# A recurrent attention block with a gated MLP behind it: the first batch's written order, its TensorE filler, the load of its states and one load's place in a queue

## Chip, cores and metric

The kernel runs on one core of a Trainium2 chip. The metric is the device time in microseconds (us) of one launch. The engines are TensorE (PE in the profile; PEld is its weight load), VectorE (DVE), ScalarE (ACT), GpSimd (POOL) and SyncE (SP), which here only issues DMAs.

## What is computed

```python
# x (8, 8, 512, 64), state (8, 8, 32, 64): batches, heads, tokens or states, width
scores  = scale * x @ state^T;  a  = softmax(scores,  -1);  xread = a @ state
scores2 = scale * state @ x^T;  a2 = softmax(scores2, -1);  sread = a2 @ x
y = concat([xread, sread], axis=2)     # 544 rows for each batch and head
y = y.transpose(0, 2, 1, 3).reshape(4352, 512)
h = y @ w_in                           # w_in (512, 2048)
sp = max(h, 0) + log1p(exp(-|h|))
out = (h * erf(sp)) @ w_out            # w_out (2048, 512)
```

x, state and out are float32. The weights come as 64-bit floats and are turned into float32 on the chip, by integer and float operations on the two words of each number.

## The kernel before

**Tiling.** All is done batch by batch, 512 tokens at a time. xread is never formed: the state of a batch is first multiplied by w_in (a "mixed" weight m, 32 states by 512 columns for each head), and the softmax weights aT then go against m. The 2048 hidden columns are cut into four groups of 512 (g or o in the code); each group's hidden values are made, go through softplus, erf and a product, and are projected by w_out into four PSUM accumulators of 128 tokens (o0 to o3). Batches 1 to 7 and the state rows use a seven-product scheme (hidden_wide L469, project_wide L610, hidden_states L527, project7 L587); the first batch does plain products.

**The first batch is a written list.** The string order0 (L1018 to L1039) holds step names; each name is a function in the dictionary do, made by step and copied (L742, L745), and running through the list emits the instructions. in_order (L81) then fixes this order on each of PE, DVE, ACT and SP, so on every engine a step can't pass the one named before it. A suffix _a puts a PSUM copy on ACT (L747), _v on DVE (L748). The names that matter:

- wN: N filler products of 128x128 (warm, L191 to L196) into a PSUM bank nobody reads.
- x0 to x3: transposes of two heads of x each (turn, L766, matmul at L770); x0_v, x1_a and so on copy them to xT. st: transposes of the first batch's states (turn_st, L775, L778), copied by st_v to st00.
- s0, s1: scores of four heads each (score, L781, matmul at L788); s00_a, s01_a, s10_a, s11_a copy them out of the two banks. tm0, tm1 turn them to tokens in rows (L795) into the two PSUM buffers named at.
- max, less, exp, sum, inv, norm with 0 or 1: softmax (L816 to L823). ta0, ta1 turn the weights (L801), ta0_a and ta1_a copy them to aT.
- i0 to i7 and o0 to o7: pieces of w_in and w_out (pieces, L731). Each has two ACT steps (a0 at L167, a1 at L169) and three DVE steps (v0 at L172, v1 at L173, v2 at L174); i0 is done in two halves, the second written i0+. get (L936) asks for the next piece from DRAM; a piece lands in one of three raw buffers, so piece n+3 can be asked for only when the v2 step of piece n is done.
- mGF: mixed weights of group G from column block F on (mixed_part, L868, matmul at L877), which takes two at buffers; mGFk_a or _v copies one half. hGI: hidden block I of group G (first, L881, matmul at L887; a third digit means one half of it). softGI, erfGI (erfGI+ for two blocks), mulGI: L917, L922, L924. pGRI: projection of block I into accumulator R (second, L890, matmul at L894). putR: copy (L900) and store of accumulator R.
- u0, u1: transposes of the other batches' states (L866). big, wt, wz, wn, tw, read: the second softmax and sread. q..., n..., cm..., ca..., lxq, lx, kept: work for batch 1, with its loads.

**Queues.** Nearly all DMAs are issued by SP, in program order. At the start these are x of batch 0 (L115, two of the four from ACT), the state of batch 0 twice (L120, once for each half of the columns, so that one transpose of 128 columns gives both halves of the partitions), three pieces of weights (L157), and the states of batches 1 to 7 (load_st, L123, L126). load_xq (L97, L102) loads the queries of a batch with 16 DMAs.

**After the first batch.** The loop over n (L1097) runs two steps for each batch 1 to 7. At n = 0 the accumulators 2 and 3 of batch 0 are still being stored: excursion(1, ..., 2, ...) does sread of batch 1, mixed weights, and attention(2), and attention(b) (L300) ends its scores with load_xq(b + 1), here load_xq(3), 16 DMAs. The two stores put2 and put3 follow (L1158, L1159). The output tile ot has three buffers, used in turn: put2, then o1, then o2 of project_wide share one ring, so that the tile o2 of n = 0 takes the buffer of put2 and o1 of n = 0 that of an earlier store. The next output additions are at L616, on DVE.

Of the kernel before, what the change touches and what calls it, by code (L numbers as in the profile page):

```python
# [9 lines left out]
F32 = mybir.dt.float32  # L10
# [7 lines left out]
def kernel(  # L18
# [17 lines left out]
    nc = tc.nc  # L36
# [70 lines left out]

    st = const.tile([P, B, P], F32, name="st")
    away0 = ring[:, 1, 0].rearrange("p k i t -> p (k i t)")
    st0 = away0[:, 512:768].rearrange("p (g k d) -> p g k d", g=2, k=2)  # L110
    x0 = xin.tile([P, NC, H, D], F32, name="x").rearrange("p c h d -> p (c h d)").rearrange(
        "p (h c d) -> p h c d", h=H, c=NC)
    x_t[0] = x0.rearrange("p h c d -> p c h d")
    for i in range(NI):
        (nc.scalar, nc.sync)[i % 2].dma_start(  # L115
            out=x0[:, 2 * i:2 * i + 2].rearrange("p h c d -> p h (c d)"),
            in_=x[0, 2 * i:2 * i + 2].rearrange("h (p c) d -> p h (c d)", c=NC))
        if i == 1:
            for k in range(2):
                nc.sync.dma_start(out=st0[:, :, k],  # L120
                                  in_=state[0].rearrange("(g h) n d -> (h n) g d", g=2))

    def load_st():  # L123
        for h in range(H):
# [63 lines left out]

    spare = ps_h.tile([P, S], F32, name="h")

    def warm(n):  # L191

        for _ in range(n):
            last = nc.tensor.matmul(out=spare[:, 0:P], lhsT=ident, rhs=ident, start=True,
                                    stop=True)
        return last  # L196

# [102 lines left out]
    def attention(b, xT, *pool, held=None):  # L300

        if held is None:
            held = {"sc": scores(b, xT, *pool)[0]}
            if b + 1 < B:
                load_xq(b + 1)
        sc = lambda e: held["sc"][:, e]
        tt = nc.vector.tensor_tensor
        turn, both = nc.vector.transpose, lambda: d["both"]
        d = {}
        a = lambda e: both()[:, e].rearrange("p (k n) -> p k n", n=Ns)  # L310

        def begin():
            d["both"] = att.tile([P, NI, S], F32, name="xT")
            d["m1"], d["z1"] = (small.tile([P, 2, NC * NI], F32, name=n) for n in ("m1", "z1"))
            d["m2"], d["z2"] = (small.tile([P, 2], F32, name=n) for n in ("m2", "z2"))
            aT[b] = keep.tile([P, 2, S], F32, name="aT")
    
        def most():
            for e in range(2):
                yield lambda e=e: (d or begin(),  # L320
                                   turn(out=both()[:, e], in_=sc(e)))
            for e in range(2):
                yield lambda e=e: nc.vector.reduce_max(out=d["m1"][:, e], in_=a(e), axis=AX.X)
            for e in range(2):
                yield lambda e=e: tt(a(e), a(e), over(d["m1"][:, e]), op=ALU.subtract)
            for e in range(2):
                yield lambda e=e: nc.vector.reduce_max(out=d["m2"][:, e:e + 1], in_=sc(e),
                                                       axis=AX.X)
            yield lambda: nc.vector.tensor_scalar(d["m2"], d["m2"], -scale, None, op0=ALU.mult)

        def exps():
            for e in range(2):
                yield lambda e=e: nc.scalar.activation(out=a(e), in_=a(e), func=ACTF.Exp,
                                                       scale=scale)
            for e in range(2):
                yield lambda e=e: nc.scalar.activation(
                    out=both()[:, 2 + e], in_=sc(e), func=ACTF.Exp, bias=d["m2"][:, e:e + 1],
                    scale=scale, accum_out=d["z2"][:, e:e + 1])

        def total():  # L340
            for e in range(2):
                yield lambda e=e: nc.vector.reduce_sum(out=d["z1"][:, e], in_=a(e), axis=AX.X)
            yield lambda: (inverse(d["z1"]), inverse(d["z2"]))

        def ready():
            for e in range(2):
                yield lambda e=e: tt(a(e), a(e), over(d["z1"][:, e]), op=ALU.mult)
            for e in range(2):
                yield lambda e=e: turn(out=aT[b][:, e], in_=both()[:, e])
            for e in range(2):  # L350
                yield lambda e=e: (turn(out=both()[:, e], in_=both()[:, 2 + e]),
                                   send() if e else None)

        def send():
            a2T = d["a2T"] = att.tile([P, 2, NC, P], F32, name="sc")
            blocks = both()[:, 0:2].rearrange("p e (c m n) -> p m (e c) n", m=NI, n=Ns)
            rows = a2T.rearrange("p e c (i n) -> p i (e c) n", n=Ns)
            for m in range(NI):
# [391 lines left out]
    def start0():  # L750
# [24 lines left out]
        def turn_st():  # L775
            held["st"] = ps_h.tile([P, 2 * P], F32, name="h")
            for g in range(2):
                nc.tensor.transpose(out=held["st"][:, P * g:P * g + P],  # L778
                                    in_=st0[:, g].rearrange("p k d -> p (k d)"), identity=ident)

        def score(g):  # L781
            if not nat:
# [73 lines left out]
    def groups0():  # L856
# [8 lines left out]
            for n, b in enumerate(bs):  # L865
                nc.tensor.transpose(out=ps_s[k][:, n], in_=st[:, b, :], identity=ident)  # L866

        def mixed_part(g, first, n):  # L868
            if (0, g) not in m_t:
                m_t[0, g] = mix.tile([P, 2, gw], F32, name="m")  # L870
            ps = ps_m[g, first] = [ps_at.tile([P, gw], F32, name="at")[:, 0:n * P]
                                   for _ in range(2)]
            for h in range(H):
                i, e = h // 2, h % 2
                r = slice(D * e, D * e + D)
                k, p = where[h]
# [29 lines left out]
        for g in range(NG):  # L906
            for first_, n in ((0, 1), (1, 1), (2, 2)) if g == 0 else ((0, 2), (2, 2)):
                step("m%d%d" % (g, first_), mixed_part, g, first_, n)
                for k in range(2):
                    copied("m%d%d%d_" % (g, first_, k),  # L910
                           lambda g=g, f=first_, n=n, k=k: m_t[0, g][:, k, P * f:P * (f + n)],
# [96 lines left out]
    for _ in range(3):  # L1008
        fetch()
    load_st()  # L1010
    for n in 8, 12:
        step("w%d" % n, warm, n)
    start0()
    groups0()
# [1 line left out]
    ready = next0()  # L1016

    order0 = """  # L1018
        w8 x1 x1_v i0a0 i0a1 x0 x0_v i0v0 i0+a1 i0+a0 st st_v i0v1 x2 x2_v x3 x3_a s0 s00_a i0+v0
        i0v2 s1 i0+v1 i0+v2 s01_a s10_a tm0 max0 less0 s11_a tm1 exp0 w12 max1 less1 sum0 i1a0  # L1020
        inv0 norm0 exp1 o0a0 m01 sum1 m011_a u0 m010_a i1a1 ta0 ta0_a inv1 norm1 m00 ta1 big1
        i1v0 m000_a get i1v1 i1v2 m001_a h000 ta1_a h01 u0_v o0v0 m02 m020_v h001 u1 m021_v h03
        h02 o1a1 o0a1 soft01 o0v1 o0v2 u1_v lxq1 soft00 erf00+ mul00 mul01 p030 get o1a0 p020
        o1v0 o1v1 o1v2 soft03 get p000 soft02 erf02+ mul02 i2a0 mul03 p001 i2a1 p010 i2v0 p031
        i2v1 i2v2 p021 i3a0 i3a1 i3v0 p002 p011 get p003 o2a1 big0 big p032 o2a0 wt0 m10 m100_v
        p012 wt1 p013 m101_v h11 soft11 h10 soft10 i3v1 i3v2 m12 m121_a xq1v wz p033 p022 wn0
        p023 o2v0 m120_v h13 o2v1 o2v2 h12 erf10+ mul10 get o3a1 wn1 get mul11 o3a0 o3v0 o3v1
        p110 soft13 soft12 o3v2 p111 erf12+ mul12 i4a0 i4a1 get get i5a0 p100 p101 p130 p131 p132
        mul13 tw0 tw0_a i4v0 i5a1 i4v1 i4v2 p102 p112 m20 m201_a m200_a p120 i5v0 i5v1 p121 p122
        h20 i5v2 o4a0 o4v0 get m22 m221_v m220_v get h21 o4a1 o4v1 o4v2 tw1 tw1_v h22 soft20 o5a0  # L1030
        o5v0 h23 p133 p123 o5a1 soft21 erf20 mul20 erf21 soft23 soft22 o5v1 mul21 p103 erf22 p200
        o5v2 p201 p220 get erf23 mul22 mul23 i6a0 i6v0 i6a1 i6v1 read read_v p113 i7a0 i7v0 i6v2
        p210 get get q q1_v p221 p230 qm1 o6a0 q0_a qm0 m30 o6v0 p222 o6a1 m301_v i7a1 p211
        m300_a o6v1 o6v2 n1 n10_a n11_v qm7 cm0 h30 n0 n01_a i7v1 qm6 h31 lx1 soft31 soft30 p202
        p203 i7v2 qm8 erf30 n00_v kept cm2 cm1 cm3 m32 m320_a p223 p231 p232 mul30 qm2 erf31 p233
        p330 m321_a qe3 h33 qm3 mul31 lxq2 o7a0 qm4 o7v0 get get p331 h32 qe2 qm5 p300 p301 qe1
        qs1 qe0 qs0 p320 p321 qs2 qr0 qr2 soft33 erf33 p212 qr1 p213 p310 p311 o7a1 ca0 qr3
        soft32 erf32 ca2 mul33 ca1 ca3 o7v1 o7v2 get mul32
    """  # L1039
    steps0 = order0.split()  # L1040
    for n, name in enumerate(steps0):
# [55 lines left out]
    for n, (b, u) in enumerate((b, u) for b in range(1, B) for u in range(2)):  # L1097
# [57 lines left out]
        if n == 0:  # L1155
            done(steps)
            excursion(1, (1, sets(1 - begins(1))), 2, lambda: erf_part(inner, inside))
            for r in 2, 3:  # L1158
                do["put%d" % r]()  # L1159
        if n == 0:  # L1160
            times_part(inner, slice(0, 1))
            times_part(inner, slice(3, 4))
# [122 lines left out]
```

## Time and profile before

| | |
|---|---|
| runs, device us | 722.75, 724.76, 1508.96 (median 724.76) |
| profiled execution: device us, span us | 722.23, 720.4 |
| granted TensorE clock, mean | 0.995 |
| all 896 + 672 matmuls of L631 | 203.0 + 161.4 us busy, 379 and 381 ns each |
| DMA | 74.70 MB, mean 104 GB/s; HBM read 49.87 MB, written 20.45 MB |

The profiled execution has its own time, 722.23 us, of which the span from its first to its last instruction is 720.4 us; 1.8 us lie outside it. A float32 product shows as two MATMUL records and a transpose as one. Matmuls overlap in the record, so sums of their durations exceed the time they take: a 128x512 record starts 0.43 us after the one before it, a 128x256 record 0.216 us, a 128x128 record 0.11 us at full clock and 0.213 us at half clock. DVE and ACT rows are start, busy time, and the wait ahead of them in brackets.

### The profile page before, as it was taken

To read this page: it belongs to the slowest core of one execution; us is meant where nothing else is said; L and a number is where in the kernel's file an instruction comes from. 1 tells how busy PE (TensorE), PEld (TensorE's weight loads), DVE (VectorE), ACT (ScalarE), POOL (GpSimd) and SP (SyncE) were. 2 spreads that over 40 slices of the span, in tenths; PEclk is the share of its full clock that TensorE was granted. 3 is DMA by queue.
4 is the path that set the end of the run, shared out by engine and by line. 5 is a ranking of instruction groups with operands and counts; after the bars stand their busy time and mean duration, and the time that the engine had idled before them with its cause. 6 is when DMAs were issued, how large, how long until landed. Compare 5 with 4: busy or idle time off the path is not lost.

```text
span 720.4 us, 10904 instructions
## 1 busy us (share of the span) xinstructions
PE 708.6 (98%) x4257; PEld 561.2 (78%) x4257; DVE 542.0 (75%) x877; ACT 374.8 (52%) x535; POOL 25.2 (3%) x34
## 2 busy tenths in 40 slices
PE   6999999999999999999999999999999999999997
PEld 6444347678878878887888878887888888889996
DVE  5897888879868988788776967697877757665533
ACT  4999695636464625545346436462464535342340
POOL 0000000000100000000000000000000000000000
PEclk8999999999999999999999999999999999999999
DMA  8956795650249163513723280615242321102101
GB/s 270 237 200 207 217 297 163 131 184 30 43 88 222 24 133 49 142 50 79 112 29 146 60 146 2 176 30 148 29 104 83 89 49 25 34 30 30 23 9 29
DMA packets 144339, 74.70 MB, mean 104 GB/s; under 512 B 123424, under 2 KB 132896, under 8 KB 142752
## 3 DMA queue, kind: packets, MB, share of 16 engines
q1 hardware_dynamic: 139520, 65.95, 33.1%
q0 software_dynamic: 4032, 7.34, 7.6%
q10 hardware_dynamic: 736, 0.72, 0.3%
q8 instruction: 33, 0.54, 0.3%
q14 instruction: 18, 0.15, 0.1%
HBM read 49.87 MB, written 20.45 MB: 98 GB/s over the span
## 4 chain that ended last, share of the span: by engine, by line
PE 89%; ACT 4%; DMA 2%; SPq 2%; DVE 2%; issue 1%; DVEq 0%; ACTq 0%
PE o L631 46%; PE h L489 13%; PE at L489 10%; PE o L894 5%; PE h L534 3%; PE o L606 3%; PE h L383 2%; PE at L383 1%; PE at L275 1%; SPq L102 1%; PE h L887 1%; ACT raw L169 1%; PE at L887 1%; DMA raw<-in_moe_w_in_dram 1%; DMA raw<-in_moe_w_out_dram 1%; SPq L75 1%
## 5 line engine op out<-in xcount | busy, mean ns | idle before, releaser
L631 PE MATMUL o<-w_out,ring 128*128 128x256 f32 x896 | 203.0, 379 | 0.0
L631 PEld LDWEIGHTS o<-w_out,ring 128*128 128x128 f32 x896 | 169.9, 190 | 24.8 <-DVE ring L1089 0.8
L631 PE MATMUL o<-raw,ring 128*128 128x256 f32 x672 | 161.4, 381 | 0.0
L631 PEld LDWEIGHTS o<-raw,ring 128*128 128x128 f32 x672 | 126.6, 190 | 25.8 <-ACT m L385 9.2
L482 ACT ACTIVATE ring<-ring 128x512 f32<-128x512 f32 x112 | 70.6, 631 | 60.5 <-DVE ring L472 59.9
L489 PE MATMUL h<-aT,m 128*128 128x256 f32 x336 | 82.2, 380 | 1.7 <-DVE ring L472 1.7
L1089 DVE TENSOR_TENSOR ring<-ring 128x1024 f32<-128x1024 f32 (+1 forms) x61 | 70.6, 1200 | 4.5 <-ACT ring L546 4.5
L489 PEld LDWEIGHTS h<-aT,m 128*128 128x128 f32 x336 | 63.7, 190 | 12.1 <-DVE ring L472 2.1
L472 DVE TENSOR_TENSOR ring<-ring,at 128x512 f32<-128x512 f32 x84 | 57.0, 679 | 16.8 <-PE at L489 15.2
L894 PE MATMUL o<-w_out,ring 128*128 128x512 f32 x128 | 59.2, 598 | 0.1
L616 DVE TENSOR_TENSOR ot<-uv,o 128x256 f32<-128x256 f32 (+1 forms) x56 | 31.0, 553 | 33.8 <-PE o L631 31.5
L472 DVE TENSOR_TENSOR ring<-ring,h 128x512 f32<-128x512 f32 x56 | 38.0, 678 | 19.7 <-PE h L489 19.6
L654 ACT COPY ot<-o 128x256 f32<-128x256 f32 x28 | 10.4, 372 | 78.9 <-PE o L631 78.9
L692 POOL DMA_DIRECT2D out_dram<-ot x28 | 24.5, 943 | 656.1 <-DVE ot L616 529.7
L894 PEld LDWEIGHTS o<-w_out,ring 128*128 128x128 f32 x128 | 23.6, 190 | 27.2 <-issue 24.6
L616 DVE TENSOR_TENSOR ot<-ot,o 128x256 f32<-128x256 f32 x56 | 22.1, 416 | 27.9 <-ACT ot L654 27.7
L504 ACT COPY ring<-h 128x512 f32<-128x512 f32 x28 | 16.4, 586 | 47.9 <-PE h L489 47.9
L663 DVE TENSOR_TENSOR ring<-ring 128x512 f32<-128x512 f32 x56 | 38.6, 689 | 1.4
L664 DVE TENSOR_TENSOR ring<-ring 128x512 f32<-128x512 f32 x56 | 36.2, 683 | 0.0
L385 ACT COPY m<-h 128x512 f32<-128x512 f32 x13 | 7.6, 586 | 46.3 <-PE h L383 46.1
L546 ACT ACTIVATE ring<-ring 128x2048 f32<-128x2048 f32 x16 | 30.5, 1904 | 0.0
L489 PE MATMUL h<-sy,sx 128*128 128x256 f32 x112 | 28.7, 379 | 0.0
(189 smaller groups left out, 958.8 us busy)
## 6 DMA issues: line engine op xcount, KB each, us to landing
w_in<-kept_in SPq DMA_DIRECT2D x7, 2048.0 KB, 8.4
raw<-in_moe_w_in_dram SPq DMA_DIRECT2D x16, 512.0 KB, 5.3
raw<-in_moe_w_out_dram SPq DMA_DIRECT2D x8, 1024.0 KB, 5.4
out_dram<-ot SPq DMA_DIRECT2D x32, 256.0 KB, 2.2
xq<-in_x_dram SPq DMA_DIRECT2D x112, 64.0 KB, 2.7
x<-in_x_dram SPq DMA_DIRECT2D x56, 128.0 KB, 3.2
out_dram<-ot POOLq DMA_DIRECT2D x28, 256.0 KB, 4.3
sc<-xT SPq DMA_DIRECT2D x112, 32.0 KB, 1.9
```

Of the source, the lines that this page charges most:

```text
L383: nc.tensor.matmul(out=ps[k][e][q, :], lhsT=st[r, b, q], rhs=of_group[g][r, :, i, :], start=True, stop=True)
L472: add = lambda o, x, y: nc.vector.tensor_tensor(o, x, y, op=ALU.add)
L482: nc.scalar.activation(out=s[k], in_=hs[k], func=ACTF.Softplus)
L489: nc.tensor.matmul(out=out[:, i], lhsT=x[:, q:q + P], rhs=y, start=(first and i == 0), stop=(i == 1), skip_group_check=not first)
L546: nc.scalar.activation(out=s, in_=s, func=ACTF.Erf)
L616: add = lambda o, x, y: tt(o, x, y, op=ALU.add)
L631: nc.tensor.matmul(out=out, lhsT=lhs[:, i, :], rhs=rhs[:, g, i, :], start=(start and i == 0), stop=(i == GF - 1), skip_group_check=not start)
L663: return [lambda: tt(S1, A21, A22, op=ALU.add), lambda: tt(S2, S1, A11, op=ALU.subtract), lambda: tt(S3, A11, A21, op=ALU.subtract), lambd ...
L664: lambda: tt(S3, A11, A21, op=ALU.subtract), lambda: tt(S4, A12, S2, op=ALU.subtract)]
L692: nc.gpsimd.dma_start(out=rows[2 * h + r][:, c], in_=ot[:, c], accum_op=ALU.add)
L894: nc.tensor.matmul(out=acc[r], lhsT=gT[g][:, i, P * r:P * r + P], rhs=w_out[:, GF * g + i, :], start=(made_of[r] == 1), stop=(made_of[r] = ...
L1089: nc.vector.tensor_tensor(s[:, ks], s[:, ks], hs[:, ks], op=ALU.mult)
```

## The change

- **Filler.** warm multiplies a constant tile of ones, which the program's preamble sets, in place of the identity, which GpSimd builds first. Steps w1 to w12 exist; the list uses w8, w3, w2, w4, w5, w5 in place of w8, w12.
- **States.** The state of batch 0 is loaded once (one DMA of 64 KB fewer on SP); turn_st makes both halves of the partitions by four plain products with the identity in place of two transposes.
- **mixed_part** can do half of its heads: the steps mGFx and mGFy. m01 and m00 are used in halves, m01 with filler between them.
- **Order.** The first half of the list, up to mul13 tw0, is new; after it only which engine takes a PSUM copy differs (m200, m320, m321, n10, n11). In the new list st_v comes ahead of the weight steps i0v; x2 goes through ACT and x3 through DVE; i0+a1 and i0+a0 change places; wt0 comes ahead of piece i3; o1a1 comes after the first erf.
- **Queries of batch 3.** attention(2) no longer calls load_xq(3); it is called after put2 and put3. On SP one of the 16 DMAs stays ahead of the two stores and 15 come behind them.

```diff
-    st0 = away0[:, 512:768].rearrange("p (g k d) -> p g k d", g=2, k=2)
+    st0 = away0[:, 512:640].rearrange("p (g d) -> p g d", g=2)
...
-            for k in range(2):
-                nc.sync.dma_start(out=st0[:, :, k],
-                                  in_=state[0].rearrange("(g h) n d -> (h n) g d", g=2))
+            nc.sync.dma_start(out=st0, in_=state[0].rearrange("(g h) n d -> (h n) g d", g=2))
...
+    ones = nc.const_aps.tensor(1.0, [P, P], F32)
...
-            last = nc.tensor.matmul(out=spare[:, 0:P], lhsT=ident, rhs=ident, start=True,
+            last = nc.tensor.matmul(out=spare[:, 0:P], lhsT=ones, rhs=ones, start=True,
...
-            if b + 1 < B:
+            if b + 1 < B and b != 2:
                 load_xq(b + 1)
...
-                nc.tensor.transpose(out=held["st"][:, P * g:P * g + P],
-                                    in_=st0[:, g].rearrange("p k d -> p (k d)"), identity=ident)
+                for k in range(2):
+                    nc.tensor.matmul(out=held["st"][D * k:D * k + D, P * g:P * g + P],
+                                     lhsT=st0[:, g], rhs=ident, start=True, stop=True)
...
-        def mixed_part(g, first, n):
+        def mixed_part(g, first, n, hs=range(H)):
...
-            for h in range(H):
+            for h in hs:
...
-        w8 x1 x1_v i0a0 i0a1 x0 x0_v i0v0 i0+a1 i0+a0 st st_v i0v1 x2 x2_v x3 x3_a s0 s00_a i0+v0
-        i0v2 s1 i0+v1 i0+v2 s01_a s10_a tm0 max0 less0 s11_a tm1 exp0 w12 max1 less1 sum0 i1a0
-        inv0 norm0 exp1 o0a0 m01 sum1 m011_a u0 m010_a i1a1 ta0 ta0_a inv1 norm1 m00 ta1 big1
-        i1v0 m000_a get i1v1 i1v2 m001_a h000 ta1_a h01 u0_v o0v0 m02 m020_v h001 u1 m021_v h03
-        h02 o1a1 o0a1 soft01 o0v1 o0v2 u1_v lxq1 soft00 erf00+ mul00 mul01 p030 get o1a0 p020
-        o1v0 o1v1 o1v2 soft03 get p000 soft02 erf02+ mul02 i2a0 mul03 p001 i2a1 p010 i2v0 p031
-        i2v1 i2v2 p021 i3a0 i3a1 i3v0 p002 p011 get p003 o2a1 big0 big p032 o2a0 wt0 m10 m100_v
-        p012 wt1 p013 m101_v h11 soft11 h10 soft10 i3v1 i3v2 m12 m121_a xq1v wz p033 p022 wn0
-        p023 o2v0 m120_v h13 o2v1 o2v2 h12 erf10+ mul10 get o3a1 wn1 get mul11 o3a0 o3v0 o3v1
...
+        w8 x1 x1_a i0a0 x0 x0_v st st_v i0a1 x3 x3_v x2 x2_a s0 s00_a w3 s1 i0v0 i0v1 i0v2 i0+a0
+        i0+v0 i0+a1 s01_v w2 tm0 i0+v1 i0+v2 max0 less0 s11_a s10_a tm1 max1 less1 i1a0 exp0 exp1
+        sum0 w4 m01x w5 m01y inv0 m010_a m011_a o0a0 w5 u0 i1a1 m00x m00y m000_a m001_a sum1 norm0
+        ta0 ta0_a inv1 norm1 ta1 ta1_a h000 i1v0 i1v1 h01 big1 i1v2 m02 o0v0 h001 m020_v o0a1 u1
+        m021_v get o1a0 o0v1 o0v2 soft01 h03 u0_v soft00 h02 erf00+ mul01 p021 p011 mul00 p000 u1_v
+        p010 o1a1 p020 p030 p001 soft03 soft02 lxq1 erf02+ o1v0 o1v1 o1v2 big0 get get mul02 i2a0
+        i2a1 mul03 big p032 i2v0 i2v1 i2v2 wt0 p031 p022 i3a0 p002 m10 i3a1 p003 i3v0 m101_v get
+        p023 o2a0 m100_v h10 p033 i3v1 wt1 get o2a1 i3v2 m12 wz xq1v p012 h11 m120_v m121_v p013 h12
+        soft10 o3a0 o2v0 o3a1 o2v1 o2v2 wn0 soft11 erf10+ mul11 h13 mul10 get soft13 p131 o3v0 o3v1
...
             for r in 2, 3:
                 do["put%d" % r]()
+            load_xq(3)
```

More of the change, by code (lines that the diff above doesn't have):

```diff
@@ L866, in turn_states @@
                 nc.tensor.transpose(out=ps_s[k][:, n], in_=st[:, b, :], identity=ident)
-        def mixed_part(g, first, n):
+        def mixed_part(g, first, n, hs=range(H)):
             if (0, g) not in m_t:
                 m_t[0, g] = mix.tile([P, 2, gw], F32, name="m")
-            ps = ps_m[g, first] = [ps_at.tile([P, gw], F32, name="at")[:, 0:n * P]
-                                   for _ in range(2)]
-            for h in range(H):
+            if 0 in hs:
+                ps_m[g, first] = [ps_at.tile([P, gw], F32, name="at")[:, 0:n * P]
+                                  for _ in range(2)]
+            ps = ps_m[g, first]
+            for h in hs:
                 i, e = h // 2, h % 2
@@ L908, in groups0 @@
                 step("m%d%d" % (g, first_), mixed_part, g, first_, n)
+                for k in range(2):
+                    step("m%d%d%s" % (g, first_, "xy"[k]), mixed_part, g, first_, n,
+                         range(4 * k, 4 * k + 4))
                 for k in range(2):
@@ L1010 @@
     load_st()
-    for n in 8, 12:
+    for n in range(1, 13):
         step("w%d" % n, warm, n)
@@ L1024 @@
-        o1v0 o1v1 o1v2 soft03 get p000 soft02 erf02+ mul02 i2a0 mul03 p001 i2a1 p010 i2v0 p031
-        i2v1 i2v2 p021 i3a0 i3a1 i3v0 p002 p011 get p003 o2a1 big0 big p032 o2a0 wt0 m10 m100_v
-        p012 wt1 p013 m101_v h11 soft11 h10 soft10 i3v1 i3v2 m12 m121_a xq1v wz p033 p022 wn0
-        p023 o2v0 m120_v h13 o2v1 o2v2 h12 erf10+ mul10 get o3a1 wn1 get mul11 o3a0 o3v0 o3v1
-        p110 soft13 soft12 o3v2 p111 erf12+ mul12 i4a0 i4a1 get get i5a0 p100 p101 p130 p131 p132
-        mul13 tw0 tw0_a i4v0 i5a1 i4v1 i4v2 p102 p112 m20 m201_a m200_a p120 i5v0 i5v1 p121 p122
@@ L1030 @@
[L1030 to L1035, printed above, removed]
@@ L1036 @@
-        p330 m321_a qe3 h33 qm3 mul31 lxq2 o7a0 qm4 o7v0 get get p331 h32 qe2 qm5 p300 p301 qe1
-        qs1 qe0 qs0 p320 p321 qs2 qr0 qr2 soft33 erf33 p212 qr1 p213 p310 p311 o7a1 ca0 qr3
-        soft32 erf32 ca2 mul33 ca1 ca3 o7v1 o7v2 get mul32
+        w8 x1 x1_a i0a0 x0 x0_v st st_v i0a1 x3 x3_v x2 x2_a s0 s00_a w3 s1 i0v0 i0v1 i0v2 i0+a0
+        i0+v0 i0+a1 s01_v w2 tm0 i0+v1 i0+v2 max0 less0 s11_a s10_a tm1 max1 less1 i1a0 exp0 exp1
+        sum0 w4 m01x w5 m01y inv0 m010_a m011_a o0a0 w5 u0 i1a1 m00x m00y m000_a m001_a sum1 norm0
@@ new lines @@
+        o3v2 soft12 get erf12+ i4a0 i4a1 wn1 p100 p130 p101 p110 get p111 mul12 i5a0 p132 mul13 tw0
+        tw0_a i4v0 i5a1 i4v1 i4v2 p102 p112 m20 m201_a m200_v p120 i5v0 i5v1 p121 p122 h20 i5v2 o4a0
+        o4v0 get m22 m221_v m220_v get h21 o4a1 o4v1 o4v2 tw1 tw1_v h22 soft20 o5a0 o5v0 h23 p133
+        p123 o5a1 soft21 erf20 mul20 erf21 soft23 soft22 o5v1 mul21 p103 erf22 p200 o5v2 p201 p220
+        get erf23 mul22 mul23 i6a0 i6v0 i6a1 i6v1 read read_v p113 i7a0 i7v0 i6v2 p210 get get q
@@ new lines @@
+        q1_v p221 p230 qm1 o6a0 q0_a qm0 m30 o6v0 p222 o6a1 m301_v i7a1 p211 m300_a o6v1 o6v2 n1
+        n10_v n11_a qm7 cm0 h30 n0 n01_a i7v1 qm6 h31 lx1 soft31 soft30 p202 p203 i7v2 qm8 erf30
+        n00_v kept cm2 cm1 cm3 m32 m320_v p223 p231 p232 mul30 qm2 erf31 p233 p330 m321_v qe3 h33
+        qm3 mul31 lxq2 o7a0 qm4 o7v0 get get p331 h32 qe2 qm5 p300 p301 qe1 qs1 qe0 qs0 p320 p321
+        qs2 qr0 qr2 soft33 erf33 p212 qr1 p213 p310 p311 o7a1 ca0 qr3 soft32 erf32 ca2 mul33 ca1 ca3
+        o7v1 o7v2 get mul32
```

## The prediction

> **What bounds the kernel.** I read the page's busy shares first, then the windows, the chain of waits, and the timeline where the windows show TensorE idle.
>
> ```profile
> PE 708.6 (98%) x4257; PEld 561.2 (78%) x4257; DVE 542.0 (75%) x877; ACT 374.8 (52%) x535; POOL 25.2 (3%) x34
> ```
>
> TensorE is busy for 708.6 of 720.4 us, fillers included. The change takes no product out of the 700 us after the start, so all it can win lies in the few places where TensorE idles or does filler. The windows (length; busy PE, PEld, DVE, ACT, POOL; granted clock; DMA share; GB/s) show them:
>
> ```profile
> 5.00:10.00 5.00, 2.28 (x42) 1.83 (x46) 2.47 (x5) 1.60 (x3) 0.00 (x0) 1.00 1.08 355
> 10.00:15.00 5.00, 3.52 (x67) 2.58 (x48) 3.77 (x7) 2.53 (x7) 0.00 (x0) 0.60 1.10 375
> 15.00:20.00 5.00, 4.91 (x44) 4.55 (x44) 4.74 (x11) 3.54 (x7) 0.00 (x0) 0.71 0.76 173
> ...
> 60.00:65.00 5.00, 4.61 (x26) 1.70 (x26) 4.83 (x5) 4.22 (x7) 0.00 (x0) 1.00 0.49 169
> ...
> 150.00:155.00 5.00, 3.34 (x16) 2.62 (x15) 4.96 (x11) 2.72 (x4) 0.00 (x0) 1.00 0.86 351
> ```
>
> Before 20 us TensorE waits, at half clock from 11.05 to 17.88 us. At 60 us it misses 0.4 us and at 150 us 1.66 us; nowhere else more than 0.3 us. The chain of waits (start, us, what) says who sets these ends:
>
> ```profile
> 15.15 4.04 PE h L194 x24
> 19.19 0.46 PE at L877 x16
> ...
> 19.67 0.43 ACT m L747 x2
> 20.11 1.06 ACT raw L169
> 21.17 0.47 ACT aT L747
> ...
> 33.89 5.66 DMA raw<-in_moe_w_out_dram
> ...
> 59.95 1.24 DVE ring L174
> 61.23 0.67 PE at L877 x16
> 61.90 2.77 PE o L894 x6
> ```
>
> The filler w12 itself is on the chain: m01 could have run when less1 freed the second at buffer (17.07 us) and ran at 19.12. From 19.67 to 61.2 the chain goes through ACT, DVE and one transfer, not through TensorE: windows of 5 us there have 4.8 to 5.0 us of ACT. Only from 61.2 us on is it TensorE. So an earlier TensorE in the first 20 us pays only as far as ACT gets earlier too. The stall at 150 us, from the timelines of DVE, SP and PE:
>
> ```profile
> 143.17 1.30 DVE L321 STREAM_TRANSPOSE xT<-sc 128x512 f32<-128x512 f32 x2
> 147.77 0.69 DVE L616 TENSOR_TENSOR ot<-uv,o 128x512 f32<-128x512 f32 x1 [3.30 <-PE o L631]
> 135.55 8.46 SPq L102 DMA_DIRECT2D xq<-in_x_dram  x16
> 144.12 1.85 SPq L694 DMA_DIRECT2D out_dram<-ot  x2
> 152.75 1.13 PE L489 MATMUL h<-aT,m 128*128 128x256 f32 x4 [1.66 <-DVE ring L472]
> ```
>
> DVE's 3.30 us are put down to PE, but the product it needs (S3, the first 8 of 24 records from 142.29 us at 0.216 us) was done near 144.2. The output tile it writes is the buffer of put2; ACT had copied put2 by 135.9, its store was issued at 144.12 behind the 16 query loads and landed at 147.65 by the trace's landing record, 0.1 us before DVE starts. Six DVE operations then stand ahead of the sum at L472 that the next product waits for.
>
> **What the Trainium skill says.** "TensorE: Matmul & The Clock Gate", Part 1, gives a free-running window of about 3.4 us: an idle one halves the clock, a busy one restores it. The trace agrees: half clock lasts 6.83 us, two windows, after a window (7.63 to 11.05) with 0.72 us of products; the window before, with 2.3 us, brought no throttle. The same page (Architectural detail) says ACT and DVE are strict FIFO; the 3.30 us that held six ready operations agree.
>
> **The change, part by part.**
>
> *Filler.* ones are set at 0.4 us, the identity at 1.31; DMA issue starts at 0.74, so w8 can start near 0.75, not 1.36, and ends near 4.2. x1 lands at 4.25. That saves 0.3 us for x1, worth nothing: ACT waits for i0 (landed 8.11) anyway. 27 filler products stand for 20, 0.21 us each warm, all in waits unless the clock halves.
>
> *One state load.* One DMA of SP (0.5 us of issue) and 64 KB go. DMA is at 1.08 to 1.10 of its share, and the two such loads and x took 0.2 to 0.7 us of landing each; I take 0.25 us earlier for all later landings (bounds 0.1 and 0.5): i0 at 7.9 and 9.4, i1 10.75 and 12.05, o0 15.05, states 17.7. Four products of two 128-column records cost 8 x 0.11 = 0.9 us for two transposes at 0.2, before x3 lands; free.
>
> *Order up to h000.* The work with its own durations, each start the later of its engine and its input. st_v no longer waits behind i0v0 on DVE: 6.3 us for 9.16. ACT: i0a0 7.9, i0a1 8.5, x2_a 9.1, s00_a 9.55 to 9.9, i0+a0 to 10.5, i0+a1 to 11.1. s1 starts after s00_a at 9.95 (before 11.65). DVE: i0v0 8.6, i0v1 9.15, i0v2 9.75, i0+v0 10.55, s01_v 10.9 to 11.3, i0+v1 11.25, i0+v2 11.95, then max0 at 12.55, where before it was 14.34 waiting for tm0. less0 13.25, max1 13.9, less1 14.6 to 15.3; exp1 to 15.9; sums and inverses in the same cadence as before, norm0 17.1, norm1 18.2 to 18.9. PE: m01x at 14.0, w5, m01y near 15.4, w5, u0 at 17.75 (states landed), m00x and m00y to 18.6. ACT: m010_a, m011_a to 16.35, o0a0, i1a1 to 18.5, m000_a and m001_a to 19.05, ta0_a to 19.7, ta1_a to 20.3 (before 22.3). h000 starts near 19.8 against 21.86: 2.0 us.
>
> *From h000 to m20.* ACT sets this. o0a1 to 21.4, then o1a0 must wait for its landing (22.08 before, 21.8 now) and ends at 22.9; table load 1.28, two softplus 1.15, table load 1.28, erf 1.06: erf00+ ends at 27.75 (before 29.4). TensorE is done with h02 at 27.7 and waits until mul01 at 28.5; before, 30.26. So 1.75 us are left, and 0.8 us are a new wait. Then o1a1 to 28.8, soft and erf to 33.5, i2 to 35.7, wt0 with its load to 37.9, i3 to 40.1, o2a0 to 41.1, wt1 42.0, o2a1 43.2. o1v2, now behind erf00+, ends at 32.7, so o2 is asked for at 32.75 (33.89 before) and lands near 38.5, covered by i3's ACT work until 40.1; without that cover each us of it would be a us. The rest of ACT's list to i4a1 has the same nine table loads, and m121_a (0.26 us) moved to DVE: i4a1 ends at 57.15 (58.67 before), i4v1 and i4v2 2.5 us later at 59.65 (61.19). m20 starts near 59.7 against 61.23: 1.5 us gained. Small stalls of TensorE within (m10 0.25, p131 0.3) lie in this. DVE, 4.8 to 4.9 of 5 us busy, takes two copies more, 0.75 us, which I place in its waits; its price uncovered would be 0.75 us.
>
> *After m20.* The list is as before but for the engine of a few copies, and before no wait shows until 150 us; the 1.5 us carry through.
>
> *Queries behind stores.* SP's 16 issues of 0.53 us shift: put2 and put3 are issued at 136.1 and 136.7 (one query load, 0.5 us, stays ahead), landing 2 us later at 138 to 139, long before DVE wants the buffer at 144.4. DVE gets 3.3 us back; the sum at L472 then waits for its own product (149.3) and TensorE's 1.66 us go: 1.7 us with bounds 1.4 and 1.8. What is queued behind: 15 query loads, 1.1 us later, used only when xq is turned after n = 1, some 40 us on; and the load of w_in, which SP reached at 146.05 and now reaches near 145.1, since the stores' wait is gone. If ACT's copies were late, SP would stand with both; they were done 8 us earlier.
>
> Sum on the profiled execution: 722.23 - 1.5 - 1.7 = 719.0 us. Its 722.23 is 0.5 and 2.5 below the two plain runs that agree (median 724.76), so I put a plain median 0.8 above: 719.8.
>
> **Rivals.**
> - *Half clock as before.* If fillers in small lots don't hold the clock, from 11.05 to 17.88 us w4 and the first w5 (18 records) cost 0.213 for 0.109 each: m01y slips from 15.4 to 17.1, m00 to 20.6 and h000 to 21.9. Only the second edit counts: 720.5, plain 721.3. For: s0 and s1 are small products. Against: the window 7.63 to 11.05 now holds about 2.1 us of work for 0.72.
> - *Landings eat the order.* o1a1's late place or the state's landing (u0 ahead of m00) costs ACT what it gained, 1.5 us, or up to 3: plain 721 to 723. For: o2's transfer was on the chain. Against: 1.6 us of slack worked out above.
> - *The stores were not the cause*, and L616 waited for PE as the view says: 1.7 us stay, 720.7, plain 721.5. The landing at 147.65 speaks against.
> - *Slower: half clock into the full stage.* If no window from 11 us on counts as busy, TensorE runs at half speed past 19.8 us; to 24.7 this costs (24.7 - 19.8)/2 = 2.45 us, of which 0.8 fills the new wait; to 31.5 it costs 5.85 - 0.8 = 5.05 and is more than the 3.2 gained: 724.1, plain 724.9. It decides from about 27.8 us on. For: w12's 24 records in one run are gone. Against: from 15 us on the fillers are 20 records in 3 us.
>
> **How the numbers follow.** Both gains as worked out 0.58; half clock as before 0.15; landings 0.13; stores not the cause 0.07; slower than before 0.07. Likeliest: 719.8 us, with 718 to 721 its own range. With the next three cases the range is 717.5 to 723.5; the top takes in most of the landing case, the bottom both upper bounds and a low plain run. A gain of 2% would be 14.5 us, nearly all of the 11.8 us in which TensorE idles (720.4 - 708.6) and the 4.25 us of w12 together; a loss of 2% needs a stall that nothing here shows. Two per cent is about what a measurement of this kernel can tell from no change. Faster 0.02, same 0.94, slower 0.04.
>
> **What would show it.** Right: h000 (first L887 row) near 20 us; no half clock between 11 and 18; m20's first L877 row on ring near 59.7; L616 near 144.5 and no PE gap at 150. Wrong: u0 or o2's piece as the releaser of ACT's waits, PE idle of over 1 us between 22 and 60, a clock below 1 after 18 us, or DVE's 3.3 us still there.

## Result

| | before | after |
|---|---|---|
| runs, device us | 722.75, 724.52, 724.76, 1508.96; median of the four 724.64, of the first three 724.52 | 719.2, 719.28, 719.83, 720.15; median 719.56 |
| profiled execution: device us, span us | 722.23, 720.4 | 720.15, 718.4 |
| granted TensorE clock, mean | 0.995 | 1.0 |

The ratio of after to before is 0.9941, with an interval of 0.9924 to 0.9957: a gain of 0.6%, some 4 us; the run of 1508.96, twice as long as the others and unexplained, is not in it. Two later measurements of the same changed kernel (after2, after3 below) gave 0.9955 and 0.9943. In the profiled pair the difference is 2.08 us.

The busy shares of after:

```profile
PE 709.6 (99%) x4277; PEld 561.7 (78%) x4277; DVE 543.6 (76%) x881; ACT 374.6 (52%) x531; POOL 25.2 (4%) x34
```

TensorE has 1.0 us more work (twenty records more, most of them filler) in a span 2.0 us shorter. The windows of after (length; busy PE, PEld, DVE, ACT, POOL; granted clock; DMA share; GB/s) say where the difference lies:

```profile
5.00:10.00 5.00, 4.07 (x60) 3.17 (x58) 2.30 (x5) 2.00 (x4) 0.00 (x0) 1.00 1.04 350
10.00:15.00 5.00, 3.76 (x60) 2.89 (x60) 4.90 (x9) 3.85 (x8) 0.00 (x0) 1.00 1.08 347
15.00:20.00 5.00, 4.51 (x60) 3.58 (x53) 4.70 (x12) 3.70 (x8) 0.00 (x0) 1.00 0.64 142
35.00:40.00 5.00, 4.26 (x10) 1.52 (x8) 4.04 (x6) 4.60 (x6) 0.00 (x0) 1.00 0.95 363
...
150.00:155.00 5.00, 5.00 (x25) 4.41 (x24) 4.42 (x9) 3.36 (x5) 0.00 (x0) 1.00 0.97 341
```

The half clock of 11 to 18 us is gone (1.00 for 0.60 and 0.71), and so is the idle TensorE at 150 us (5.00 for 3.34). New is a hole at 35 to 40 us, 4.26 of 5. The chain of waits of after (start, us, what) names it:

```profile
29.66 5.63 DMA raw<-in_moe_w_in_dram
35.37 1.14 ACT w_in L165
36.52 1.06 ACT raw L167
37.59 1.24 DVE w_in L171
38.85 1.24 DVE w_in L172
40.13 0.67 PE at L880 x16
...
61.12 0.67 PE at L880 x16
61.78 2.77 PE o L897 x6
```

L165 and L167 are the two ACT steps of a weight piece, L171 and L172 two of its DVE steps, L880 the mixed products, L890 the first and L897 the projection (L167, L169, L173, L174, L877, L887 and L894 in before). The piece is i2. Its second half, which landed at 35.29 us by the trace's landing record, sets ACT, then DVE, then m10 at 40.13. From there on the chain is TensorE, where in before it ran through ACT and DVE up to 61.2 us. m20, the row at 61.12, had stood at 61.23 in before: of the 1.5 us forecast for the first batch, 0.1 came in this execution. Nearly all of the 2.08 us is the stall at 150, of which the timelines of SP, DVE and PE of after show:

```profile
136.22 0.91 SPq L694 DMA_DIRECT2D out_dram<-ot  x2
...
144.29 0.65 DVE L616 TENSOR_TENSOR ot<-uv,o 128x512 f32<-128x512 f32 x1
...
149.36 0.69 DVE L472 TENSOR_TENSOR ring<-ring,h 128x512 f32<-128x512 f32 x1 [0.79 <-PE h L489]
149.95 1.89 PE L489 MATMUL h<-aT,m 128*128 128x256 f32 x8
```

In before the same sum stood here:

```profile
152.02 0.68 DVE L472 TENSOR_TENSOR ring<-ring,h 128x512 f32<-128x512 f32 x1
```

The stores are issued at 136.22 for 144.12, L616 starts without a wait, the sum at L472 starts 2.7 us earlier and waits for its own product only, and the next product follows without a bracket, so without a wait.

### The profile page after: what moved, and what is told of

Its sections match the earlier page's. It is cut to its first block, busy times and chain, and to the rows that moved or that the text cites. A ratio compares the mean times of both kernels' runs of the same rounds, so it can differ in the third digit from the quotient of the medians.

```text
span 718.4 us, 10943 instructions
## 1 busy us (share of the span) xinstructions
PE 709.6 (99%) x4277; PEld 561.7 (78%) x4277; DVE 543.6 (76%) x881; ACT 374.6 (52%) x531; POOL 25.2 (4%) x34
## 4 chain that ended last, share of the span: by engine, by line
PE 94%; SPq 2%; DMA 2%; DVE 1%; ACT 1%; issue 0%; DVEq 0%; ACTq 0%
PE o L631 47%; PE h L489 13%; PE at L489 10%; PE o L897 7%; PE h L534 3%; PE o L606 3%; PE h L383 2%; DMA raw<-in_moe_w_in_dram 2%; PE at L383 2%; PE h L890 2%; SPq L102 2%; PE at L890 1%; PE at L275 1%; PE at L880 1%; PE o L224 1%; DVE w_in L172 0%
## 5 line engine op out<-in xcount | busy, mean ns | idle before, releaser
L482 ACT ACTIVATE ring<-ring 128x512 f32<-128x512 f32 x112 | 70.6, 631 | 59.7 <-DVE ring L472 59.1
L489 PE MATMUL h<-aT,m 128*128 128x256 f32 x336 | 81.9, 379 | 0.0
L489 PEld LDWEIGHTS h<-aT,m 128*128 128x128 f32 x336 | 63.8, 190 | 10.1 <-issue 1.4
L472 DVE TENSOR_TENSOR ring<-ring,at 128x512 f32<-128x512 f32 x84 | 57.1, 680 | 16.9 <-PE at L489 15.2
L897 PE MATMUL o<-w_out,ring 128*128 128x512 f32 x128 | 59.5, 599 | 0.4 <-DVE ring L930 0.4
L472 DVE TENSOR_TENSOR ring<-ring,h 128x512 f32<-128x512 f32 x56 | 38.0, 678 | 21.4 <-PE h L489 21.3
L616 DVE TENSOR_TENSOR ot<-uv,o 128x256 f32<-128x256 f32 (+1 forms) x56 | 31.0, 553 | 30.4 <-PE o L631 28.1
L897 PEld LDWEIGHTS o<-w_out,ring 128*128 128x128 f32 x128 | 23.6, 190 | 27.6 <-issue 24.8
L616 DVE TENSOR_TENSOR ot<-ot,o 128x256 f32<-128x256 f32 x56 | 22.2, 416 | 27.9 <-ACT ot L654 27.7
L504 ACT COPY ring<-h 128x512 f32<-128x512 f32 x28 | 16.5, 588 | 47.9 <-PE h L489 47.9
L495 ACT COPY ring<-h 128x512 f32<-128x512 f32 x28 | 16.4, 587 | 24.0 <-PE h L489 24.0
```

What stands on the lines that cost most here:

```text
L472: add = lambda o, x, y: nc.vector.tensor_tensor(o, x, y, op=ALU.add)
L482: nc.scalar.activation(out=s[k], in_=hs[k], func=ACTF.Softplus)
L489: nc.tensor.matmul(out=out[:, i], lhsT=x[:, q:q + P], rhs=y, start=(first and i == 0), stop=(i == 1), skip_group_check=not first)
L616: add = lambda o, x, y: tt(o, x, y, op=ALU.add)
L897: nc.tensor.matmul(out=acc[r], lhsT=gT[g][:, i, P * r:P * r + P], rhs=w_out[:, GF * g + i, :], start=(made_of[r] == 1), stop=(made_of[r] = ...
```

## The experiments

My theory after the result: the gain is the wait for put2's store; the first batch's new order itself works as forecast, but i2's landing decides what of it is left. The rivals: the gain comes from the fillers (the clock), from the one load of the states, or from the first batch as a whole. The first four kernels undo one part each or do one alone.

**q_only**: before, with only the queries of batch 3 moved behind the stores.

```diff
-            if b + 1 < B:
+            if b + 1 < B and b != 2:
...
+            load_xq(3)
```

> The kernel before with one edit alone: the queries of batch 3 are loaded behind the stores of put2 and put3. If the store was what held DVE at 144.4 us, DVE's 3.30 us at L616 and TensorE's 1.66 us at 150 us go, and the time falls by 1.7 to 1.9 us against the kernel before (ratio near 0.9975), whatever the first batch does. If L616 waited for its product, as the view of waits says, nothing moves and the 1.66 us stay.

Measured: 720.28 us (7 runs, 719.52 to 721.97) beside 722.58 of before; ratio 0.9968 (0.9958 to 0.9979). In its profile L616 has no wait and TensorE no gap at 150 us:

```profile
146.00 0.65 DVE L616 TENSOR_TENSOR ot<-uv,o 128x512 f32<-128x512 f32 x1
```

That execution, at 721.97 us, is the slowest of the seven, since its first batch came late (m20 at 62.83 us for 61.23). This one edit carries most of the gain.

**no_q**: after, with the queries put back ahead of the stores.

```diff
-            if b + 1 < B and b != 2:
+            if b + 1 < B:
...
-            load_xq(3)
```

> The kernel after without that edit: queries of batch 3 ahead of the stores again, all else as changed. If the edit is worth 1.7 to 1.9 us by itself, this is slower than the kernel after by that much, near 721.4, and keeps what the first batch gained: 0.1 us of the profiled executions (m20 at 61.1 against 61.2), but up to 3 us of the plain medians (724.6 to 719.6 less 1.9). If the first batch gains nothing, it is at the kernel before, 722.2 to 724.6.

Measured: 724.54 us (18 runs, 720.11 to 727.47); ratio 1.0019 (1.0007 to 1.0031). The whole work on the first batch, alone, gains nothing. Its timeline:

```profile
145.41 0.91 SPq L694 DMA_DIRECT2D out_dram<-ot  x2
...
148.74 0.69 DVE L616 TENSOR_TENSOR ot<-uv,o 128x512 f32<-128x512 f32 x1 [3.69 <-DMA out_dram<-ot]
```

Here the view names the store as the releaser, where the first profile of before had named PE.

**no_fill**: after without w3, w2, w4, w5 and w5.

```diff
-s00_a w3 s1 ... s01_v w2 tm0 ... sum0 w4 m01x w5 m01y ... o0a0 w5 u0
+s00_a s1 ... s01_v tm0 ... sum0 m01x m01y ... o0a0 u0
```

> The kernel after without w3, w2, w4, w5 and w5 (w8 stays). If the fillers hold the clock, half clock comes back for 6.8 us or more somewhere between 11 and 25 us; what is left of TensorE's work there is small before h000, so h000 moves by at most 1 us, and every us of half clock past 21 us costs half a us until ACT's chain hides it: 0 to 3 us over the kernel after. If the clock does not depend on them, h000 comes earlier, since m01y no longer stands behind ten filler records (1.1 us), and the time is the same or up to 0.5 us lower.

Measured: 719.5 us (719.01 to 720.35); ratio 0.9956 (0.9944 to 0.9968). The clock did fall, as its windows show:

```profile
10.00:14.00 4.00, 3.35 (x40) 2.10 (x40) 3.65 (x8) 3.23 (x7) 0.00 (x0) 0.57 1.07 402
14.00:17.00 3.00, 0.84 (x16) 0.37 (x16) 2.90 (x7) 1.63 (x5) 0.00 (x0) 1.00 0.90 157
17.00:21.00 4.00, 3.36 (x28) 2.47 (x28) 3.81 (x8) 3.02 (x5) 0.00 (x0) 0.57 1.02 290
```

0.57 over 4 us is half clock for (1 - 0.57) x 4 / 0.5 = 3.4 us, twice (10.44 to 13.85 us and 17.27 to 20.68 by the clock's own records). The plain runs show no loss. The profile shows a cost all the same, which early landings hid (o0 landed at 15.54, for 16.75 in after). These are u0 and h000 of after:

```profile
18.62 0.63 PE L867 MATMUL o<-ident,st 128*128 128x128 f32 x4 [0.49 <-DMA st<-in_state_dram]
20.89 2.84 PE L890 MATMUL h<-aT,m 128*128 128x512 f32 x6 [0.24 <-ACT aT L747]
```

And these of no_fill:

```profile
17.64 1.09 PE L867 MATMUL o<-ident,st 128*128 128x128 f32 x4 [1.11 <-DMA st<-in_state_dram]
21.06 2.84 PE L890 MATMUL h<-aT,m 128*128 128x512 f32 x6
```

From u0 to h000 no_fill takes 3.42 us for 2.27, and its chain of waits is TensorE's from u0 to m20. So the second stretch of half clock does stand in the way there; the table below prices it. "TensorE: Matmul & The Clock Gate", Part 1, of the Trainium skill gives a free-running window of about 3.4 us; each of the two stretches agrees.

**two_loads**: after with the states of batch 0 loaded twice and two transposes for the four products.

```diff
-            nc.sync.dma_start(out=st0, in_=state[0].rearrange("(g h) n d -> (h n) g d", g=2))
+            for k in range(2):
+                nc.sync.dma_start(out=st0[:, :, k],
+                                  in_=state[0].rearrange("(g h) n d -> (h n) g d", g=2))
...
```

> The kernel after with the state of batch 0 loaded twice and turned by two transposes again. One more DMA of 64 KB ahead of all weights: if landings bound the first 20 us, i0 lands about 0.25 us later (bounds 0.1 to 0.5) and h000 with it; since m20 hangs on later landings too, 0 to 0.5 us over the kernel after, which may not be told from nothing.

Measured: 720.06 us (719.78 to 720.4); ratio 0.9962 (0.9951 to 0.9974). The two halves of i0 landed at 8.05 and 9.81 us (8.57 and 9.93 in after). The one load can't be told from nothing.

The four say where the gain is, not yet why no_q loses all of the first batch's lead, nor whether the store's buffer is the cause or only the order of SP. The second set asks that, and whether i2 could land earlier.

**after2**: after once more, as the yardstick of this set.

> The kernel after, unchanged, once more beside the others. If the landings of the first weights vary from execution to execution (i0 from 8.1 to 9.0 us, i2 from 33.2 to 36.0 us at its second half in the profiles so far), then h000 and m20 move with them here too: m20 between 59.7 and 61.2, TensorE's wait at 39 us between 0.15 and 1.0. The time 719 to 720.5.

Measured: 720.12 us (718.9 to 722.77); ratio 0.9955 (0.9942 to 0.9967).

**no_q_uv**: no_q, with put2 copied into a buffer of another ring. SP's order stays that of no_q; only L616 no longer takes the buffer that put2's store holds.

```diff
-            ot = outs.tile([P, d_model], F32, name="ot", bufs=3)
+            ot = outs.tile([P, d_model], F32, name="uv") if r == 2 else \
+                outs.tile([P, d_model], F32, name="ot", bufs=3)
```

> The kernel after with the queries of batch 3 ahead of the stores again, but put2 copied into a buffer of uv, so that o2 of n = 0 takes a buffer whose store (put1) was issued 20 us earlier. SP's order is that of no_q. If the wait for put2's store through the shared buffer is the whole cost of no_q, DVE's 3.7 us at L616 and TensorE's 2.2 us at 151 us go and the time and its spread are those of the kernel after, 719.2 to 720.5. If SP's order itself costs (the 16 loads, or the load of w_in behind them), it stays at 722 to 725.

Measured: 720.17 us (719.53 to 721.7); ratio 0.9958 (0.9941 to 0.9975). Its timeline:

```profile
144.93 0.65 DVE L616 TENSOR_TENSOR ot<-uv,o 128x512 f32<-128x512 f32 x1
145.06 0.43 SPq L694 DMA_DIRECT2D out_dram<-uv  x1
...
150.60 1.89 PE L489 MATMUL h<-aT,m 128*128 128x256 f32 x8
```

The store is issued as late as ever (145.06), after DVE has already started L616, and nobody waits. So the queue's order costs nothing by itself; the shared buffer behind it does.

**no_q2** and **no_q3**: no_q again, the first timed beside the others, the second for one more profile.

> The kernel of no_q once more, for the spread of its times (720.1 to 727.5 in 18 runs) and a second profile. If the spread is that of the store's landing, this profile's time less that of the kernel after is TensorE's wait at 151 us plus what the first weights' landings differ, and the wait is longer the later the store lands.

> The kernel of no_q a third time, for one more profile. The wait at L616 ends with the landing of put2's store; when TensorE comes earlier through the first batch, the store does not, and the wait at 150 us grows by as much (2.8 us at m20 59.7, 2.2 us at m20 61.8 so far).

Measured: no_q2 724.32 us (721.64 to 727.28); ratio 1.0012 (0.9996 to 1.0028). no_q3, one run: 723.29. The execution profiled in no_q2 had early landings, and its timeline has the first batch's two ends where the prediction put them:

```profile
19.90 2.84 PE L890 MATMUL h<-aT,m 128*128 128x512 f32 x6 [0.24 <-ACT aT L747]
...
59.70 0.67 PE L880 MATMUL at<-ring 64*32 64x256 f32 x16
...
147.18 0.69 DVE L616 TENSOR_TENSOR ot<-uv,o 128x512 f32<-128x512 f32 x1 [4.24 <-DMA out_dram<-ot]
...
152.16 1.13 PE L489 MATMUL h<-aT,m 128*128 128x256 f32 x4 [2.60 <-DVE ring L472]
```

h000 at 19.90 (forecast 19.8), m20 at 59.70 (forecast 59.7). But 1.53 us earlier at m20 than before has become 0.59 us at L489 (152.16 against 152.75), since the wait for the store grew from 3.30 to 4.24 us. The device time, 721.64 against 722.23, differs by the same 0.59. The store was issued at 143.35 for 144.12 and landed at 147.05 for 147.65: it follows TensorE's lead only in part.

**i2_first**: after, with i2 asked for ahead of the 16 query loads of batch 1 (lxq1).

```diff
-soft03 soft02 lxq1 erf02+ o1v0 o1v1 o1v2 big0 get get mul02
+soft03 soft02 get lxq1 erf02+ o1v0 o1v1 o1v2 big0 get mul02
```

> The kernel after with piece i2 asked for ahead of the 16 query loads of batch 1 on SP (i3 stays behind them). If i2's landing behind those loads is what ate the first batch's gain, i2 is asked for near 23 us and lands by 30, ACT no longer idles 0.8 us at 35, TensorE's wait at 39 us falls from 1.0 to under 0.3, and m20 comes 0.8 us earlier, near 60.3; the time falls by 0.5 to 1.0 us against the kernel after. If ACT's own work is the bound, m20 stays at 61.1 and the time too. A loss is possible if the query loads, now ending near 33 us, push i3's landing past 39 us.

Measured: 723.47 us (14 runs); ratio 1.000 (0.9989 to 1.0011). i2 landed at 29.46 and its wait was gone, but the query loads then kept i3 until 41.59, and TensorE waited for that:

```profile
44.25 3.01 PE L890 MATMUL h<-aT,m 128*128 128x512 f32 x4 [2.21 <-DVE m L748]
```

Four records in 3.01 us (1.72 to 1.91 in after) show half clock behind the wait; m20 came at 64.62.

**i2_split**: the query loads of batch 1 in two lots of eight, with i2 ahead of the first lot and i3 ahead of the second.

```diff
-    def load_xq(b):
+    def load_xq(b, hs=range(H)):
...
-soft03 soft02 lxq1 erf02+ o1v0 o1v1 o1v2 big0 get get mul02
+soft03 soft02 get lxq1 get lxq1b erf02+ o1v0 o1v1 o1v2 big0 mul02
```

> The kernel after with the 16 query loads of batch 1 in two lots of 8: i2 is asked for ahead of the first lot, i3 ahead of the second. i2 lands by 30 us, i3 near 34 to 35, so that neither ACT (0.8 us at 35) nor TensorE (1.0 to 2.1 us at 39) waits for them, and m20 is set by ACT's list alone: 59.7 to 60.3, 0.8 us before the kernel after on the average, time 719.2 to 719.5. If ACT's list or the first weights' landings are the whole bound, nothing is gained. A loss if o2's piece, now behind the second lot, lands past 41.7 us.

Measured: 723.13 us (22 runs); ratio 0.9987 (0.9979 to 0.9996). i2 landed at 29.90 and i3 at 37.83, and now o2 was late:

```profile
45.01 1.14 ACT L165 ACTIVATE w_out<-raw 128x1024 f32<-128x1024 f32 x1 [4.90 <-DMA raw<-in_moe_w_out_dram]
...
50.14 4.11 PE L890 MATMUL at<-aT,m 128*128 128x512 f32 x5 [2.57 <-DVE m L748]
```

The wait moves to the next piece: neither place for i2's request beats the changed kernel, and the gains expected of both did not come.

**after3** and **before2**: both kernels once more, for their profiles.

> The kernel after once more, as the reference of the other three. 719 to 720.5; m20 at 59.7 when the second half of i2 lands near 33.9 us and at 61.1 when it lands near 35.2, as in the profiles so far.

> The kernel before once more, for a second profile. With landings as late as in the other profiles (i0 8.4 or later, i2 at 34.5 or later), its m20 comes at 62.5 to 63, as in the kernel with the queries' edit alone (62.8), and not at 61.2 as in its first profile; the first batch's order is then worth 1.5 us at equal landings. If m20 is at 61.2 again with late landings, the order is worth nothing there.

Measured: after3 720.17 us (719.1 to 720.68); ratio 0.9943 (0.9928 to 0.9958). before2, one run: 722.39. Its landings (i0's first half 8.25, i2 32.67) were not as late as the expectation asks, so it doesn't try that case. It names the store as the releaser, though, for before itself:

```profile
147.86 0.69 DVE L616 TENSOR_TENSOR ot<-uv,o 128x512 f32<-128x512 f32 x1 [3.60 <-DMA out_dram<-ot]
```

In all five profiles that have this wait, L616 starts 0.12 or 0.13 us after the landing of put2's store (147.65, 147.74, 148.62, 147.05 and 148.75 us in before, before2, no_q, no_q2 and no_q3).

**All profiles in one table.** i2 is the landing of its second half; m20 the first L880 (L877) row on ring; the last column is the profiled device time less m20. In two_loads the lines are a little further down.

| kernel | i2 landed | m20 | m20 - i2 | L616 waits | device | device - m20 |
|---|---|---|---|---|---|---|
| before | 33.24 | 61.23 | 27.99 | 3.30 | 722.23 | 661.00 |
| before2 | 32.67 | 61.02 | 28.35 | 3.60 | 722.39 | 661.37 |
| no_q | 35.95 | 61.81 | 25.86 | 3.69 | 723.11 | 661.30 |
| no_q2 | 33.86 | 59.70 | 25.84 | 4.24 | 721.64 | 661.94 |
| no_q3 | 36.06 | 61.91 | 25.85 | 3.73 | 723.29 | 661.38 |
| q_only | 34.57 | 62.83 | 28.26 | none | 721.97 | 659.14 |
| after | 35.29 | 61.12 | 25.83 | none | 720.15 | 659.03 |
| after2 | 35.24 | 61.11 | 25.87 | none | 720.12 | 659.01 |
| after3 | 34.45 | 60.28 | 25.83 | none | 719.26 | 658.98 |
| two_loads | 34.88 | 60.73 | 25.85 | none | 719.89 | 659.16 |
| no_q_uv | 35.94 | 61.77 | 25.83 | none | 720.82 | 659.05 |
| no_fill | 33.22 | 60.02 | 26.80 | none | 719.01 | 658.99 |
| i2_first | 29.46 | 64.62 | 35.16 | none | 723.69 | 659.07 |
| i2_split | 29.90 | 64.14 | 34.24 | none | 723.21 | 659.07 |

Two constants come out. Without the store's wait, what lies behind m20 takes 658.98 to 659.16 us in all nine profiles, whatever came ahead; with it, 1.9 to 2.9 us more, and most where m20 was earliest. And in the new order m20 follows i2's landing by 25.83 to 25.87 us in eight executions of four kernels, so such an execution is as fast as i2's landing allows, over a range of 2.2 us. Where i2's request keeps its place, no_fill is the one exception: i2 landed at 33.22, and m20 came 26.80 us later, since TensorE at half clock had fallen behind. By the constant, 33.22 + 25.85 = 59.07 was within reach, so an estimate of what half clock cost in this execution is 0.95 us.

The three profiles of the old order allow a rough look at what the new one is worth at like landings. Their chains of waits don't come straight from i2, yet m20 lies 27.99 to 28.35 us behind it. With i2 at 34.45 (after3) m20 is at 60.28; with i2 at 34.57 (q_only), at 62.83. But the new order also lands later: o0 landed at 15.28, 15.46 and 15.76 us in the three profiles of the old order, and later than any of these in nine of the eleven of the new one (15.02 to 17.40). So most of what the order gains is taken back: apart from i2_first and i2_split, m20 comes at 59.70 to 61.91 us in the new order and at 61.02 to 62.83 in the old.

## Why the prediction was right, and where its sum was not

The total, 719.8 us, agrees with the measured 719.56, 720.12 and 720.17, the wait for the store is shown by experiment, and the first batch reached its forecast in one profile (no_q2). That the number fits so well is partly luck: the sum for the profiled execution was 719.0 and came to 720.15, 1.15 too low, and the plain median was put 0.8 above it and came 0.6 below, so the two errors made up for each other.

- **Queries behind stores: right in cause, and the larger part.** Forecast 1.7 us with bounds of 1.4 and 1.8. The last column gives 661.00 - 659.05 = 1.95 us in the first profile of before and 2.32 in the second. That the releaser was put2's store and not PE was argued in the prediction; no_q_uv shows it, by taking the buffer alone away. The bound of 1.8 was too narrow: it took TensorE's gap of that one execution. (Seven operations, not six, stand on DVE between L616 and the sum at L472.)
- **The offset to plain runs: mis-sized.** I put 0.8 us for both kernels. The medians of after are within 0.9 us of its profiled executions on either side, but those of before (722.58 to 724.64) lie 0.2 to 2.4 above its profiled ones, and no_q's 1.4 and 2.7. In the plain runs of one set, taking the store's wait away from no_q2 is worth 724.32 - 720.17 = 4.2 us (no_q_uv), where the profiles show 1.9 to 2.9. So the excess goes with the wait for the store. No profile caught one of the executions of 725 to 727 us, so how late the store lands in them stays open.
- **First batch: the order right, the landings wrong.** Forecast 1.5 us at m20; the profiled pair gave 0.1, after3 0.95, no_q2 1.53, no_q a loss of 0.6. The step that failed is "I take 0.25 us earlier for all later landings". i0's first half landed at 8.57 where it said 7.9 (8.11 in before), o0 at 16.75 for 15.05, i2 at 35.29. In no_q2 (o0 15.02, i2 33.86) h000 and m20 came within 0.1 us of the forecast, though i0 landed at 8.26 for 7.9. The one load of the states, the ground for the 0.25 us, moved nothing that two_loads can show. This is the rival "landings eat the order": in after m20 is 1.4 us later than in no_q2, and so is i2, a piece that the rival didn't name. TensorE was late as well, since u0 waited for the state, as the rival feared, and h000 came at 20.89 for 19.8. It then waited 0.87 us for i2 ahead of m10; without that wait m20 would, by difference, have been at 60.25, still 0.55 late.
- **What the first batch is worth in plain runs.** In one set q_only had 720.28 us, two_loads 720.06 and no_fill 719.5, so 0.2 to 0.8 us on top of the queries, with intervals that overlap. An estimate from the constants agrees: 719.56 to 720.17, less 659.05, puts m20 at 60.5 to 61.1 us, against 720.28 - 659.14 = 61.1 in q_only, so 0 to 0.6 us. Alone it is worth nothing (no_q, no_q2): where m20 was earlier, in no_q2, most of the lead turned into a longer wait for the store. Within the order, the halves of mixed_part, the earlier w8 and the copies that changed engine were never tried apart.
- **The new wait ahead of p021: 0.8 us forecast**, 0.41 us in after (the row at 29.55 us of the projection, L897). It cost nothing further, because i2's landing came later and set m20 in any case.
- **Filler: right that the clock would hold** (1.00 from 5.5 us on), and the rival of half clock fell for this kernel. Its price is open: the prediction put 1.5 us on a half clock up to 18 us, and no_fill, with two such stretches up to 20.7 us, lost some 0.95 us in its profile by the estimate above and nothing that its plain runs show. Its i2 was also asked for at 27.25 us, 1.1 us or more before those with the fillers (28.34 to 30.36); whether that comes from the missing fillers wasn't tried.
- **o2's request:** covered, as forecast, with 1.1 us of slack for 1.6 (landed at 40.54, used at 41.67 in after). i2_split shows what is lost without it. The prediction looked at o2 and o1; the piece to follow was i2, the first one behind the 16 query loads of batch 1.
- **Two more readings of before were off, without consequence.** The window from 4.22 to 7.63 us held 2.70 us of products, not 2.3. And TensorE's idle time past 20 us isn't only at 60 and 150 us: 3.8 us of it lie after 700 us, where the change does nothing.

Why i2's landing differs between executions is shown one step back only. In the profiles with the fillers, and with i2's request in its place, it comes 18.2 to 19.3 us after o0's, and o0's landing varies from 15.02 to 17.40: the first of its sixteen parts is in at 13.5 to 14.4, and the last one lags 1.0 to 3.6 us behind it (1.2 to 1.6 in the old order). The Trainium skill, "DMA: Bandwidth & Descriptors", section "Why a DMA increments its semaphore by 16 and not by 1", says that a DMA runs on up to 16 engines which finish independently and has landed only with the last; the landing records agree. An instruction fetch of 16 KB runs on one engine at 13.8 to 15.1 us in the new order (14.26 us, for 1.79 us, in after) and at 15.4 to 15.95 in the old one. That it makes the lagging part late is an argument from the times; it wasn't tried.

## What to carry to other kernels

A store queued behind a run of loads holds its buffer: look for who takes that buffer next, and break either link, the queue's order or the shared buffer; both gave the same time here. Time won ahead of such an event can be given back at it (0.94 of 1.53 us in no_q2), so remove the later wait first and only then judge an earlier gain. An order fitted to the landings of one execution is worth what those landings repeat: plot the point of interest against the landing over several profiles before you count its gain. The same holds for a kernel that leaves something out: no_fill looked free of cost until its landings were set beside the others'.

## What the hardware showed that I had not expected

- Half clock followed waits of TensorE of 2.21 us (i2_first, 45.06 to 48.48 us) and 2.57 us (i2_split, 50.53 to 53.95). The 3.4 us just before held 1.21 and 0.85 us of products. In no_fill the stretches before half clock held 1.12 and 0.84 us, in before 0.72. The 3.4 us from 4.22 us in before, with 2.70 us of products, brought no half clock.
- A view's releaser can differ between two executions of one kernel: L616 in before is put down to PE (3.30 us) in one and to the store (3.60 us) in the other.
- With half clock for 6.8 us in its first 21, no_fill has the fastest profiled time of all, 719.01 us; its i2 landed earlier than in any other execution of the new order that leaves i2's request in its place.
